# Eight instead of ten rows of w2 in every partition, and the other 352 rows as one load of 88 partitions

## The chip, the core and the metric

The kernel runs on one core of a Trainium2 chip. The metric is the device time of one execution in microseconds (us); the figure for the kernel before is the median of three timed runs, 344.06 us. A profile of one further execution gives a span (first to last instruction) and a trace with every instruction, every DMA packet and every increment of a DMA semaphore.

The engines are named as in the profile: PE multiplies matrices (PEld is its weight load), DVE, ACT and POOL are the vector, scalar and general engines, SP only issues DMAs here. "SPq" is the queue of DMAs that SP issues. A core has 16 DMA engines; one load is dealt out over several of them, each with its own share of the rows, and each of them reports to the load's semaphore when its share has landed.

## The reference

Two batch rows of one token pass through attention with a cache and through a small feed-forward block, and a gate mixes the two:

```python
q = (x @ wq)                       # [2, 4096] -> 32 heads of 128
scores = einsum(q, k_cache) * 128 ** -0.5        # k_cache [2, 32, 4096, 128]
o = einsum(softmax(scores), v_cache)             # v_cache [2, 32, 4096, 128]
a = o.reshape(2, 1, 4096) @ wo                   # wo [4096, 512]
h = maximum(B_x @ w1, 0)                         # w1 [512, 1376]
b = h @ w2                                       # w2 [1376, 512]
out = g * a + (1 - g) * b                        # g = sigmoid(sum(x * gate_w))
```

The weights and caches are bf16. Nearly all of the 145.43 MB that are read are the two caches (64 MB each, in MB of 2^20 bytes). In the kernel B_x is not read: the reference calls the feed-forward block with x too. The piece of work that matters here is `b = h @ w2`: its contraction runs over 1376 rows of w2, each of 512 bf16 numbers, that is 1 KB.

## The kernel before

**Loads.** SP issues all large loads in one order (lines 325 to 339): wq, w1, ten pieces of the key cache (L329), nine pieces of the value cache (L329, numbered v0 to v8, the last two of 4 MB), then the rows of w2 that are called `w2x` (L332, two loads), then wo in two parts (L334, L336), and last the shared part of w2 in three (L338: w2b, w2c, w2d). Each load waits for the region of SBUF that it overwrites; the w2 loads of L338 wait until the last piece but two of the value cache (v6) has been read by PE.

**w2 in two parts.** The contraction over 1376 rows is done 128 rows at a time. Rows 96 to 1375 are the shared part: 128 partitions by ten rows, loaded as seven, two and one row per partition (w2b, w2c, w2d). Rows 0 to 95 are `w2x`: 24 partitions by four rows, in two loads of 12 partitions each, at partitions 0 to 11 and 32 to 43. POOL has cleared the whole of `w2x` before (L710), so that the other partitions add nothing.

**The feed-forward rows.** `ffn_h` (L438) multiplies x with w1 in four column groups c and four depth steps t into one PSUM row block that DVE has cleared (L439): 16 matmuls of 320 columns for the shared rows, and 8 of 48 columns for the rows of `w2x` (groups 0 and 1 alone), the latter with the weights that PE already holds (`mm_held`, whose records stand under L477). `ffn_relu` (L457) transposes the result (L458, 448 columns) and writes `hT`, [128, 14, 2]: 14 columns of 128 contraction rows, ten for the shared part, four for `w2x`, for two batch rows.

**The end.** When the last value piece (v8) has been multiplied, `project(range(-4, 0))` (L663) adds the four `w2x` steps into PSUM, `o_gather`, `o_scale` and `o_turn` finish the heads, and `project(range(24))` multiplies with the first part of wo, 24 matmuls at L670 that wait for `wo0`. `pr_copy` (L675) copies this sum to SBUF. `last_rows` (L684) then adds, in groups of four matmuls (`fin_row`, L679): eight rows of the second part of wo (waiting for `wo1`), the copied sum, and the ten shared rows of w2, waiting for w2b before row 0, w2c before row 7 and w2d before row 9. Two DVE and two ACT copies (L698, L700) and one DMA store the result.

Of the kernel before, what the change touches and what calls it, by code (L numbers as in the profile page):

```python
# [3 lines left out]
dt = mybir.dt  # L4
# [6 lines left out]
DFF = 1376  # L11
# [5 lines left out]
REGION = {"A": 0, "Ah": HALF, "B": 2 * HALF, "Bh": 3 * HALF, "C": 4 * HALF}  # L17
# [104 lines left out]
def bass_gated_mix__gqa_block_cached__dense_activation_relu__decode_kernel(  # L122
# [18 lines left out]
    sb = nc.alloc_sbuf_tensor  # L141
# [11 lines left out]
    kv = sb("kv", [128, 5 * HALF], dt.bfloat16)  # L153
    xTw = sb("xTw", [128, 4, 32], dt.bfloat16)
    qrow = sb("qrow", [128, 2, 4, 128], dt.bfloat16)
    wreg = kv[:, REGION["C"]:REGION["C"] + HALF]
    w1 = kv[:, REGION["B"]:REGION["B"] + 4 * DFF]
    w2 = kv[:, REGION["Ah"]:REGION["Ah"] + 10 * 512].rearrange("p (r n) -> p r n", n=512)
    kt = sb("kt", [128, NKT, 2048], dt.float32)
    kt16 = kt[:, :, :].rearrange("p k n -> p (k n)").bitcast(dt.bfloat16).rearrange(  # L160
        "p (k g r par s two) -> p k g r par s two", k=NKT, g=2, par=2, s=16, two=2)
# [10 lines left out]
    w2x = kt_late[:, 13824:15872].rearrange("p (j n) -> p j n", n=512)  # L172
# [14 lines left out]
    s4 = sb("s4", [32, 4, 128], dt.bfloat16)  # L187
    O_sb = sb("O_sb", [32, 2, 128], dt.bfloat16)
    oW = sb("oW", [128, 32, 2], dt.bfloat16)
    hT = sb("hT", [128, 14, 2], dt.bfloat16)  # L190
    out_sb = sb("out_sb", [2, 512], dt.bfloat16)
    hrowT = kt[:, 2, 0:448]

    PSF = nc.alloc_psum_tensor("PS", [128, 4096], dt.float32)
    PSB = PSF[:, :].bitcast(dt.bfloat16)
# [3 lines left out]
    def psf(p0, p1, c0, n):  # L199
        return PSF[p0:p1, c0:c0 + n]  # L200

    BANK = 512
# [4 lines left out]
    QR_B = 2  # L207
    QT_B = 4
    G_C0 = MISC + 64
    HR_C0 = 6 * BANK - 320  # L210
    XT_B0 = 2 * (MISC + 400)
    L_C0 = MISC + 96
    O_C0 = MISC + 128
# [7 lines left out]
    sem = {n: nc.alloc_semaphore("sem_" + n) for n in names}  # L221
# [9 lines left out]
    def marker(name):  # L231
        m = mk.get(name)
        if m is None:
            m = _Marker()
            mk[name] = m
        return m
# [29 lines left out]
    def dve(fn, waits=(), signal=None, dwaits=()):  # L266
        P.add("dve", fn, waits=[marker(w) for w in waits], signal=marker(signal) if signal else None, dwaits=dwaits)
# [4 lines left out]
    def pe(fn, waits=(), signal=None, dwaits=()):  # L272
        P.add("pe", fn, waits=[marker(w) for w in waits], signal=marker(signal) if signal else None, dwaits=dwaits)
# [5 lines left out]
         waits=["c_i16z"], signal="c_i16")  # L279
# [8 lines left out]
         waits=["c_s1"], signal="c_s2")  # L288
    pool(lambda g: g.affine_select(out=sell_odd, in_=sell_odd, pattern=[[4, 8], [32, 4]],
                                   compare_op=ALU.is_ge, fill=0.0, base=3, channel_multiplier=-1),  # L290
         waits=["c_s2"], signal="c_sell")
# [3 lines left out]
         waits=["c_m1"], signal="c_m2")  # L295
    pool(lambda g: g.affine_select(out=mask8[:], in_=mask8[:], pattern=[[16, 8]],
                                   compare_op=ALU.is_ge, fill=0.0, base=15, channel_multiplier=-1),
         waits=["c_m2"], signal="c_mask8")
# [3 lines left out]
         waits=["c_s4z"], signal="c_s4")  # L302
# [2 lines left out]
    wq_in = A_wq.rearrange("(p t) n -> p (t n)", t=4)  # L305
    w1_in = B_w1.rearrange("(p t) f -> p (t f)", t=4)
    wo_in = A_wo.rearrange("(p r) n -> p (r n)", r=32)
    w2_in = B_w2[96:1376, :].rearrange("(p r) n -> p r n", r=10)
    w2x_in = B_w2[0:96, :].rearrange("(a i e j) n -> a e i (j n)", a=2, i=4, e=3)
    k_rows = A_k_cache.rearrange("b h s d -> (b h s) d")  # L310
    v_rows = A_v_cache.rearrange("b h s d -> (b h s) d")

# [7 lines left out]
    def sp(fn, waits=(), dwaits=()):  # L320
        P.add("sp", fn, waits=waits, dwaits=dwaits)
# [5 lines left out]
    for kind, n, u, halves, region in pieces:  # L327
        sp(lambda e, kind=kind, n=n, u=u, halves=halves, region=region:
           e.dma_start(piece_sb(halves, region), piece_in(kind, u, halves)).then_inc(landed[kind, n][0], 16),  # L329
           waits=[marker(m) for m in predecessor[kind, n]])  # L330
    for a in range(2):
        sp(lambda e, a=a: e.dma_start(w2x[32 * a:32 * a + 12, :, :].rearrange("p j n -> p (j n)"), w2x_in[a]).then_inc(sem["w2x"], 16),  # L332
           waits=[marker("c_w2x")])
    sp(lambda e: e.dma_start(wreg[:, 0:512 * WO_CUT], wo_in[:, 0:512 * WO_CUT]).then_inc(sem["wo0"], 16),  # L334
       waits=[marker(holder["C"][0])])
    sp(lambda e: e.dma_start(wreg[:, 512 * WO_CUT:HALF], wo_in[:, 512 * WO_CUT:HALF]).then_inc(sem["wo1"], 16))  # L336
    for name, r0, r1 in (("w2b", 0, 7), ("w2c", 7, 9), ("w2d", 9, 10)):
        sp(lambda e, name=name, r0=r0, r1=r1: e.dma_start(w2[:, r0:r1, :], w2_in[:, r0:r1, :]).then_inc(sem[name], 16),  # L338
           waits=[marker(holder["Ah"][0])])
    sp(lambda e: e.dma_start(out.rearrange("b s n -> (b s) n"), out_sb[:, :]).then_inc(sem["out"], 16),  # L340
# [56 lines left out]
    def x_rows(e, out, c, t, rhs, held):  # L397
        if held:
            return mm_held(e, out, xTw[:, t, :], rhs, t == 0, t == 3, (128, 32), (0, 32 * c))
        return e.matmul(out, lhsT=xTw[:, t, :], rhs=rhs, start=(t == 0), stop=(t == 3), tile_position=(0, 32 * c))  # L400
# [35 lines left out]
            q_place(k)  # L436

    def ffn_h():  # L438
        dve(lambda v: v.memset(psf(0, 128, HR_C0, 448), 0.0), signal="dve_h0")  # L439
        for t in range(4):  # L440
            for c in range(4):
                def fn(e, t=t, c=c):
                    rhs = w1[:, t * DFF + 96 + 320 * c:t * DFF + 416 + 320 * c].rearrange("p (i j) -> p j i", j=10)
                    out = psf(32 * c, 32 * c + 32, HR_C0, 320).rearrange("p (j i) -> p j i", j=10)
                    return x_rows(e, out, c, t, rhs, False)
                first = t == 0 and c == 0
                pe(fn, dwaits=([(sem["w1"], 16)] if first else []), waits=(["dve_h0"] if first else []))
                if c < 2:
                    def fnx(e, t=t, c=c):
                        rhs = w1[:, t * DFF + 48 * c:t * DFF + 48 * c + 48].rearrange("p (i e j) -> p j e i", i=4, e=3)  # L450
                        out = psf(32 * c, 32 * c + 32, HR_C0 + 320, 128).rearrange("p (j k) -> p j k", j=4)[:, :, 0:12].rearrange(
                            "p j (e i) -> p j e i", e=3)
                        return x_rows(e, out, c, t, rhs, True)
                    pe(fnx)
        P.ops["pe"][-1].marker = marker("pe_h")

    def ffn_relu():  # L457
        dve(lambda v: v.transpose(out=hrowT, in_=psf(0, 128, HR_C0, 448)), waits=["pe_h"], signal="dve_hrT")  # L458
        for b in range(2):
            dve(lambda v, b=b: v.tensor_scalar(out=hT[:, :, b], in0=hrowT[:, b:448:32], scalar1=0.0,  # L460
                                               scalar2=gm[:, b:b + 1], op0=ALU.max, op1=ALU.mult),
                waits=["dve_hrT", "dve_gm"], signal=f"dve_h{b + 1}")

# [200 lines left out]
    def project(rows):  # L664
        for r in rows:
            t = r % 4
            lhsT, rhs = (hT[:, 14 + r, :], w2x[:, t, :]) if r < 0 else (oW[:, r, :], wreg[:, r * 512:(r + 1) * 512])
            dw = {-4: [(sem["w2x"], 32)], 0: [(sem["wo0"], 16)]}.get(r, [])
            waits = {-4: ["dve_h2", "dve_pr0"], 0: ["dve_oW"]}.get(r, [])
            pe(lambda e, t=t, r=r, lhsT=lhsT, rhs=rhs: e.matmul(psf(32 * t, 32 * t + 2, PR_C0, 512), lhsT=lhsT, rhs=rhs,  # L670
                                                               start=(r < 0), stop=(r >= WO_CUT - 4), tile_position=(0, 32 * t)),
               dwaits=dw, waits=waits, signal=("pe_pr" if r == WO_CUT - 1 else None))
# [4 lines left out]
    def fin_row(first, last, lhsT, rhs, dw, waits, signal):  # L677
        for c in range(4):
            pe(lambda e, c=c: e.matmul(psf(32 * c, 32 * c + 2, FIN_C0, 128), lhsT=lhsT, rhs=rhs[:, c * 128:(c + 1) * 128],  # L679
                                       start=first, stop=last, tile_position=(0, 32 * c), skip_group_check=True),  # L680
               dwaits=(dw if c == 0 else []), waits=(waits if c == 0 else []), signal=(signal if c == 3 else None))

    def last_rows():
        for r in range(WO_CUT, 32):  # L684
            fin_row(r == WO_CUT, False, oW[:, r, :], wreg[:, r * 512:(r + 1) * 512], [(sem["wo1"], 16)] if r == WO_CUT else [], [], None)
        fin_row(False, False, sel2[:, :], pr_sb, [], ["dve_pr", "dve_sel2"], None)
        for r in range(10):
            dw = {0: [(sem["w2b"], 16)], 7: [(sem["w2c"], 16)], 9: [(sem["w2d"], 16)]}.get(r, [])
            fin_row(False, r == 9, hT[:, r, :], w2[:, r, :], dw, [], "pe_fin" if r == 9 else None)

    def store():
        def piece(c):
# [10 lines left out]
    gate()  # L703
    q_proj()
    ffn_h()
    ffn_relu()
    for i in range(64):
        k_turn(i)
# [22 lines left out]
    v_unit(last)  # L731
    v_extract(last)
    project(range(-4, 0))
    o_gather(1, (last,))
    o_scale(1)
    o_turn()
    project(range(WO_CUT))
    pr_copy()
    last_rows()
    store()  # L740

# [31 lines left out]
```

## Time and profile before

| What | us |
|---|---|
| median of three runs (343.96 to 344.13) | 344.06 |
| profiled execution, device time | 344.31 |
| its span, first to last instruction | 343.0 |
| span in which the three w2 loads of L338 are under way, from the last issue | 319.32 to 340.92 |
| last four matmuls, copies, store, after that | 340.96 to the end |

Busy times over the span: PE 220.4, DVE 197.2, PEld 52.7, POOL 13.9, ACT 10.2 us. The mean traffic is 424 GB/s. No engine that computes is busy for more than 64% of the span; the DMA engines' row in the page's 40 slices has no slice under eight tenths but the last.

Two kinds of record in the trace are used below beside the page. The packet records give start, duration, size and queue of every DMA packet, but not the engine. The semaphore records give the time of every increment; a load that is dealt out over k engines shows k increments at landing times. In this profile an increment comes some 0.4 us after the last packet of its engine.

### The profile page before, as it was taken

How to read it: one execution, taken by the hardware profiler on the slowest of the kernel's cores; microseconds unless marked ns; L12 is line 12 of the kernel's file. 1: busy time of each engine (PE TensorE's matmuls, PEld its weight loads, DVE VectorE, ACT ScalarE, POOL GpSimd, SP SyncE). 2: the span in 40 equal slices, each digit the busy share in tenths (PEclk: the TensorE clock that was granted, in tenths of full speed). 3: DMA queues.
4: the chain of work that ended last, by engine and by line, in shares of the span. 5: the costliest groups of instructions: out<-in, count | busy, mean ns of one | idle time of the engine just before them, and what ended most of it. 6: DMA issues, size and time to landing. Idle time of an engine off the chain costs nothing.

```text
span 343.0 us, 2384 instructions
## 1 busy us (share of the span) xinstructions
PE 220.4 (64%) x1236; PEld 52.7 (15%) x764; DVE 197.2 (57%) x140; ACT 10.2 (3%) x30; POOL 13.9 (4%) x38
## 2 busy tenths in 40 slices
PE   0454629889969799799799463709073542809655
PEld 0110101111111111111111121102020110202312
DVE  0247249899889899698999496230606041110621
ACT  1060000000000000000000120000000000000000
POOL 6000000000000000000000200000000000000000
PEclk9986958999989999989899966967858595876968
DMA  8998989899999999898999999898989999999995
GB/s 314 451 495 367 489 367 489 374 481 436 420 466 390 429 428 481 374 489 371 485 420 436 451 405 468 382 481 374 481 382 481 420 436 451 405 420 432 412 418 213
DMA packets 3789, 145.50 MB, mean 424 GB/s; under 512 B 427, under 2 KB 560, under 8 KB 840
## 3 DMA queue, kind: packets, MB, share of 16 engines
q1 hardware_dynamic: 3778, 145.43, 98.4%
q8 instruction: 4, 0.07, 0.1%
q14 instruction: 1, 0.01, 0.0%
q10 hardware_dynamic: 6, 0.00, 0.0%
HBM read 145.43 MB, written 0.00 MB: 424 GB/s over the span
## 4 chain that ended last, share of the span: by engine, by line
DMA 59%; DVE 19%; PE 17%; issue 4%; ACT 0%; SPq 0%; DVEq 0%
DMA kv<-in_A_v_cache_dram 25%; DMA kv<-in_A_k_cache_dram 24%; DVE kt L471 16%; PE PS L477 7%; DMA kv<-in_B_w_dram 6%; PE PS L603 4%; DMA kv<-in_A_wq_dram 4%; PE PS L498 2%; PE PS L582 2%; PE PS L400 1%; DVE qrow L424 1%; DVE mpad L514 1%; ACT kt L526 0%; PE PS L484 0%; DVE kt L530 0%
## 5 line engine op out<-in xcount | busy, mean ns | idle before, releaser
L471 DVE STREAM_TRANSPOSE kt<-kv 128x2048 f32<-128x2048 f32 x64 | 141.2, 2274 | 24.5 <-DMA kv<-in_A_k_cache_dram 24.5
L498 PE MATMUL PS<-kt,qbuf 128*128 128x512 bf16 x256 | 107.0, 418 | 32.0 <-issue 27.2
L477 PE MATMUL PS<-kt,qbuf 128*128 128x512 bf16 x256 | 106.9, 418 | 0.0
L603 PE MATMUL PS<-kv,kt 128*64 128x512 bf16 x192 | 46.5, 462 | 56.7 <-DMA kv<-in_A_v_cache_dram 56.7
L615 DVE TENSOR_TENSOR kt<-PS,maskc 32x512 f32<-32x512 f32 (+1 forms) x21 | 14.5, 689 | 89.8 <-PE PS L477 82.2
L498 PEld LDWEIGHTS PS<-kt,qbuf 128*128 128x128 bf16 x256 | 25.9, 101 | 141.5 <-issue 141.5
L477 PE MATMUL PS<-kv,kt 128*64 128x512 bf16 x192 | 45.9, 456 | 0.0
L603 PEld LDWEIGHTS PS<-kv,kt 128*64 128x64 bf16 x192 | 14.9, 132 | 96.4 <-issue 96.4
L582 PE MATMUL PS<-kv,kt 128*32 128x512 bf16 x128 | 11.5, 522 | 10.3 <-DVE kt L543 7.3
L555 DVE TENSOR_TENSOR kt<-kt,mask 128x2048 bf16<-128x2048 bf16 (+1 forms) x10 | 16.1, 1654 | 0.0
L395 POOL TENSOR_TENSOR qbuf<-qs,mask 128x64 bf16<-128x64 bf16 x16 | 6.5, 406 | 162.2 <-PE PS L477 145.6
L627 DVE TENSOR_REDUCE kt<-kt 128x128 f32<-128x512 f32 x9 | 9.2, 1019 | 0.3
L526 ACT ACTIVATE kt<-PS,negm 128x512 bf16<-128x512 f32 x4 | 2.7, 685 | 172.8 <-DVE negm L522 172.8
L400 PE MATMUL PS<-kv,xTw 128*32 128x512 bf16 (+1 forms) x32 | 5.3, 693 | 3.5 <-DMA kv<-in_A_wq_dram 3.5
L582 PEld LDWEIGHTS PS<-kv,kt 128*32 128x32 bf16 x128 | 4.7, 125 | 16.3 <-DVE kt L543 7.8
L424 DVE CAST qrow<-PS 128x256 bf16<-128x256 f32 x2 | 2.6, 1508 | 5.7 <-PE PS L477 5.7
L643 PE MATMUL PS<-kt,selx 128*32 128x128 f32 x18 | 2.9, 293 | 4.0 <-DVE kt L627 3.0
L347 PE MATMUL PS<-ident,x_sb 3*128 3x3 bf16 x4 | 0.3, 167 | 8.2 <-DMA x_sb<-in_gate_w_dram 8.2
L350 DVE COPY xT<-PS 128x12 bf16<-128x12 bf16 x1 | 0.2, 171 | 8.5 <-PE PS L347 8.5
L700 ACT ACTIVATE out_sb<-PS 2x128 bf16<-2x128 f32 x2 | 0.5, 270 | 142.3 <-PE PS L679 142.2
L514 DVE TENSOR_REDUCE mpad<-PS 128x2 f32<-128x2048 f32 x1 | 2.3, 2291 | 3.1 <-PE PS L510 3.1
L477 PE MATMUL PS<-kv,xTw 128*32 128x512 bf16 (+1 forms) x24 | 3.7, 512 | 0.0
(78 smaller groups left out, 45.2 us busy)
## 6 DMA issues: line engine op xcount, KB each, us to landing
kv<-in_A_k_cache_dram SPq DMA_DIRECT2D x4, 4096.0 KB, 29.4
kv<-in_A_v_cache_dram SPq DMA_DIRECT2D x2, 4096.0 KB, 24.4
kv<-in_A_wq_dram SPq DMA_DIRECT2D x1, 4096.0 KB, 12.5
kv<-in_A_wo_dram SPq DMA_DIRECT2D x1, 3072.0 KB, 34.2
kv<-in_B_w_dram SPq DMA_DIRECT2D x1, 1376.0 KB, 15.3
kv<-in_A_wo_dram SPq DMA_DIRECT2D x1, 1024.0 KB, 36.2
kv<-in_B_w_dram SPq DMA_DIRECT2D x1, 896.0 KB, 21.4
kv<-in_B_w_dram SPq DMA_DIRECT2D x1, 256.0 KB, 21.7
```

Of the source, the lines that this page charges most:

```text
L395: pool(lambda g: g.tensor_tensor(out=out, in0=src, in1=mask, op=ALU.mult).then_inc(sem_q[k % 2], 1), waits=waits)
L400: return e.matmul(out, lhsT=xTw[:, t, :], rhs=rhs, start=(t == 0), stop=(t == 3), tile_position=(0, 32 * c))
L424: dve(lambda v, dst=dst, src=src: v.tensor_copy(out=dst, in_=src), waits=[f"pe_qr{half}"], signal=f"qrow{half}{e2}")
L471: dve(lambda v: v.transpose(out=dst, in_=pairs[:, h, 64 * a:64 * a + 64, :]).then_inc(sem_kt[i % SPAN], 1), waits=([f"pe_sc_{i - NKT}"] if ...
L477: return e.add_instruction(mybir.InstMatmult(start_tensor_calc=start, stop_tensor_calc=stop, tile_size=size, tile_position=at, ldweights=F ...
L498: ins = e.matmul(out, lhsT=lhsT, rhs=rhs, start=False, stop=False)
L514: dve(lambda v: v.tensor_reduce(out=mpad[:, 0:2], in_=psf(0, 128, 0, 4 * BANK).rearrange("p (par n) -> p par n", par=2), axis=AX.X, op=ALU ...
L555: ins = v.tensor_tensor(out=out, in0=src.unsqueeze(2).to_broadcast(shape), in1=mask8[:].unsqueeze(1).unsqueeze(3).to_broadcast(shape), op= ...
L582: ins = e.matmul(psf(32 * t, 32 * t + 32, V_BS[n] * BANK, 512), lhsT=v_weights(n)[:, j], rhs=rows[:, :, j, :], start=(j < 4), stop=(j >= n ...
L603: ins = e.matmul(out, lhsT=lhsT, rhs=rows[:, :, k, :], start=start, stop=stop, tile_position=(0, 64 * t))
L615: dve(lambda e: e.tensor_tensor(out=parts[p0:p1], in0=psf(p0, p1, bank * BANK, 512).rearrange("p (c d) -> p c d", c=4), in1=maskc[p0:p1].u ...
L627: dve(lambda e: e.tensor_reduce(out=X2[:, b, k, :], in_=parts.rearrange("p c d -> p d c"), axis=AX.X, op=ALU.add), waits=[f"dve_m{n}"], si ...
```

## The change

The shared part gets eight rows per partition (rows 352 to 1375), loaded as five, two and one. The other 352 rows come as one load of 88 partitions by four rows, partitions 0 to 87. The feed-forward matmuls follow: 16 of 256 columns, and 12 (in groups 0, 1, 2) of 128, 128 and 96 columns; `hT` has 12 columns instead of 14, and the last stage adds eight rows of w2 instead of ten.

```diff
-    w2 = kv[:, REGION["Ah"]:REGION["Ah"] + 10 * 512].rearrange("p (r n) -> p r n", n=512)
+    w2 = kv[:, REGION["Ah"]:REGION["Ah"] + 8 * 512].rearrange("p (r n) -> p r n", n=512)
...
-    w2_in = B_w2[96:1376, :].rearrange("(p r) n -> p r n", r=10)
-    w2x_in = B_w2[0:96, :].rearrange("(a i e j) n -> a e i (j n)", a=2, i=4, e=3)
+    w2_in = B_w2[352:1376, :].rearrange("(p r) n -> p r n", r=8)
+    w2x_in = B_w2[0:352, :].rearrange("(p j) n -> p (j n)", j=4)
...
-    for a in range(2):
-        sp(lambda e, a=a: e.dma_start(w2x[32 * a:32 * a + 12, :, :].rearrange("p j n -> p (j n)"), w2x_in[a]).then_inc(sem["w2x"], 16),
-           waits=[marker("c_w2x")])
+    sp(lambda e: e.dma_start(w2x[0:88, :, :].rearrange("p j n -> p (j n)"), w2x_in).then_inc(sem["w2x"], 16), waits=[marker("c_w2x")])
...
-    for name, r0, r1 in (("w2b", 0, 7), ("w2c", 7, 9), ("w2d", 9, 10)):
+    for name, r0, r1 in (("w2b", 0, 5), ("w2c", 5, 7), ("w2d", 7, 8)):
...
-        dve(lambda v: v.memset(psf(0, 128, HR_C0, 448), 0.0), signal="dve_h0")
+        dve(lambda v: v.memset(psf(0, 128, HR_C0, 384), 0.0), signal="dve_h0")
...
-                    rhs = w1[:, t * DFF + 96 + 320 * c:t * DFF + 416 + 320 * c].rearrange("p (i j) -> p j i", j=10)
+                    rhs = w1[:, t * DFF + 352 + 256 * c:t * DFF + 608 + 256 * c].rearrange("p (i j) -> p j i", j=8)
...
-                if c < 2:
+                if c < 3:
                     def fnx(e, t=t, c=c):
-                        rhs = w1[:, t * DFF + 48 * c:t * DFF + 48 * c + 48].rearrange("p (i e j) -> p j e i", i=4, e=3)
+                        n = min(32, 88 - 32 * c)
+                        rhs = w1[:, t * DFF + 128 * c:t * DFF + 128 * c + 4 * n].rearrange("p (i j) -> p j i", j=4)
...
-        dve(lambda v: v.transpose(out=hrowT, in_=psf(0, 128, HR_C0, 448)), waits=["pe_h"], signal="dve_hrT")
+        dve(lambda v: v.transpose(out=hrowT, in_=psf(0, 128, HR_C0, 384)), waits=["pe_h"], signal="dve_hrT")
...
-            dw = {-4: [(sem["w2x"], 32)], 0: [(sem["wo0"], 16)]}.get(r, [])
+            dw = {-4: [(sem["w2x"], 16)], 0: [(sem["wo0"], 16)]}.get(r, [])
...
-        for r in range(10):
-            dw = {0: [(sem["w2b"], 16)], 7: [(sem["w2c"], 16)], 9: [(sem["w2d"], 16)]}.get(r, [])
-            fin_row(False, r == 9, hT[:, r, :], w2[:, r, :], dw, [], "pe_fin" if r == 9 else None)
+        for r in range(8):
+            dw = {0: [(sem["w2b"], 16)], 5: [(sem["w2c"], 16)], 7: [(sem["w2d"], 16)]}.get(r, [])
+            fin_row(False, r == 7, hT[:, r, :], w2[:, r, :], dw, [], "pe_fin" if r == 7 else None)
```

More of the change, by code (lines that the diff above doesn't have):

```diff
@@ L189, in bass_gated_mix__gqa_block_cached__dense_activation_relu__decode_kernel @@
     oW = sb("oW", [128, 32, 2], dt.bfloat16)
-    hT = sb("hT", [128, 14, 2], dt.bfloat16)
+    hT = sb("hT", [128, 12, 2], dt.bfloat16)
     out_sb = sb("out_sb", [2, 512], dt.bfloat16)
-    hrowT = kt[:, 2, 0:448]
+    hrowT = kt[:, 2, 0:384]
     PSF = nc.alloc_psum_tensor("PS", [128, 4096], dt.float32)
@@ L209, in bass_gated_mix__gqa_block_cached__dense_activation_relu__decode_kernel @@
     G_C0 = MISC + 64
-    HR_C0 = 6 * BANK - 320
+    HR_C0 = 6 * BANK - 256
     XT_B0 = 2 * (MISC + 400)
@@ L442, in fn @@
                 def fn(e, t=t, c=c):
-                    rhs = w1[:, t * DFF + 96 + 320 * c:t * DFF + 416 + 320 * c].rearrange("p (i j) -> p j i", j=10)
-                    out = psf(32 * c, 32 * c + 32, HR_C0, 320).rearrange("p (j i) -> p j i", j=10)
+                    rhs = w1[:, t * DFF + 352 + 256 * c:t * DFF + 608 + 256 * c].rearrange("p (i j) -> p j i", j=8)
+                    out = psf(32 * c, 32 * c + 32, HR_C0, 256).rearrange("p (j i) -> p j i", j=8)
                     return x_rows(e, out, c, t, rhs, False)
@@ L447, in ffn_h @@
                 pe(fn, dwaits=([(sem["w1"], 16)] if first else []), waits=(["dve_h0"] if first else []))
-                if c < 2:
+                if c < 3:
                     def fnx(e, t=t, c=c):
-                        rhs = w1[:, t * DFF + 48 * c:t * DFF + 48 * c + 48].rearrange("p (i e j) -> p j e i", i=4, e=3)
-                        out = psf(32 * c, 32 * c + 32, HR_C0 + 320, 128).rearrange("p (j k) -> p j k", j=4)[:, :, 0:12].rearrange(
-                            "p j (e i) -> p j e i", e=3)
+                        n = min(32, 88 - 32 * c)
+                        rhs = w1[:, t * DFF + 128 * c:t * DFF + 128 * c + 4 * n].rearrange("p (i j) -> p j i", j=4)
+                        out = psf(32 * c, 32 * c + 32, HR_C0 + 256, 128).rearrange("p (j i) -> p j i", j=4)[:, :, 0:n]
                         return x_rows(e, out, c, t, rhs, True)
@@ L457, in ffn_relu @@
     def ffn_relu():
-        dve(lambda v: v.transpose(out=hrowT, in_=psf(0, 128, HR_C0, 448)), waits=["pe_h"], signal="dve_hrT")
+        dve(lambda v: v.transpose(out=hrowT, in_=psf(0, 128, HR_C0, 384)), waits=["pe_h"], signal="dve_hrT")
         for b in range(2):
-            dve(lambda v, b=b: v.tensor_scalar(out=hT[:, :, b], in0=hrowT[:, b:448:32], scalar1=0.0,
+            dve(lambda v, b=b: v.tensor_scalar(out=hT[:, :, b], in0=hrowT[:, b:384:32], scalar1=0.0,
                                                scalar2=gm[:, b:b + 1], op0=ALU.max, op1=ALU.mult),
@@ L666, in project @@
             t = r % 4
-            lhsT, rhs = (hT[:, 14 + r, :], w2x[:, t, :]) if r < 0 else (oW[:, r, :], wreg[:, r * 512:(r + 1) * 512])
-            dw = {-4: [(sem["w2x"], 32)], 0: [(sem["wo0"], 16)]}.get(r, [])
+            lhsT, rhs = (hT[:, 12 + r, :], w2x[:, t, :]) if r < 0 else (oW[:, r, :], wreg[:, r * 512:(r + 1) * 512])
+            dw = {-4: [(sem["w2x"], 16)], 0: [(sem["wo0"], 16)]}.get(r, [])
             waits = {-4: ["dve_h2", "dve_pr0"], 0: ["dve_oW"]}.get(r, [])
```

## The prediction

> **What bounds the kernel now.** I read the page's slices and its chain of waits first, because they say which resource ends last.
>
> ```profile
> DMA  8998989899999999898999999898989999999995
> q1 hardware_dynamic: 3778, 145.43, 98.4%
> DMA 59%; DVE 19%; PE 17%; issue 4%; ACT 0%; SPq 0%; DVEq 0%
> ```
>
> The DMA engines are busy from the first slice to the last but one, and transfers fill the largest share of the chain. SP issues early enough that their queue never runs dry. So a load's size matters only through the moment at which the last of the 16 DMA engines finishes its last share. The end of the chain in order of time shows this:
>
> ```profile
> 319.32 21.59 DMA kv<-in_B_w_dram
> 340.96 0.26 PE PS L679 x4
> 341.21 0.02 issue
> 341.24 0.28 DVE out_sb L698
> ```
>
> The last load of L338 (w2d) lands at 340.92, and only four matmuls, the copies and the store come after it. Next I cut the end into short windows (columns: PE, PEld, DVE, ACT, POOL busy, granted clock, DMA share, GB/s):
>
> ```profile
> 337.00:338.00 1.00, 1.00 (x16) 0.30 (x12) 0.00 (x0) 0.00 (x0) 0.00 (x0) 0.51 0.97 386
> 338.00:339.00 1.00, 0.64 (x40) 0.46 (x36) 0.69 (x1) 0.00 (x0) 0.00 (x0) 1.00 0.63 243
> 339.00:340.00 1.00, 0.36 (x12) 0.07 (x16) 0.00 (x0) 0.00 (x0) 0.00 (x0) 1.00 0.39 129
> 340.00:341.00 1.00, 0.85 (x40) 0.48 (x40) 0.00 (x0) 0.00 (x0) 0.00 (x0) 1.00 0.05 18
> ```
>
> The DMA share falls from 0.97 to 0.05 over three microseconds: the engines do not finish together. The semaphore records say by how much. w2d's sixteen increments come at 338.74 to 339.05 (eight), then 339.24, 339.65, 339.81, 340.01, 340.26, 340.56, 340.76 and 340.92. The end waits for the last one.
>
> **Why they are apart.** w2x's semaphore has only six landing increments, 326.25 to 327.30, three for each load: its 24 packets of 4,096 B went to three engines, four and four each. Linking packets end to start, they stand 0.156 us apart, so each of the three lost 8 x 0.156 = 1.25 us; they are the ones at 339.81, 340.01 and 340.26 (their wo0 increments, 334.17, 334.35, 334.62, come 7.31 us after 326.86, 327.04, 327.30). The three that finish last, 340.56 to 340.92, carry no w2x. They were already late when v8 landed (327.61, 327.81, 327.96, while eleven engines landed between 325.63 and 326.09). Their lateness began at the 16 KB packets of queue 8 (instructions) at 24.67, 209.61 and 323.12: after the third, a 32,768 B packet starting at 324.127 took 1.764 us instead of 1.214. Each fetch fell on another engine and cost it about 1.5 us for good.
>
> **The change, part by part.**
>
> *Feed-forward rows.* The columns are the same in sum: 16 x 320 + 8 x 48 = 16 x 256 + 4 x 352 = 5,504. There are four matmuls more. By the held 48-column row (268 ns each) they cost at most 4 x 0.27 = 1.1 us, at least nothing. This line covers it:
>
> ```profile
> 24.47 5.78 issue
> ```
>
> PE idles for 5.78 us before the first scores, because the first key piece lands only at 27.81. The shorter memset and transpose (448 to 384 columns; the transpose takes 0.65 us, so some 0.09 less) lie in the same gap. The third key piece overwrites w1 and waits for these matmuls, but its load stands behind 12 MB that land until about 47 us, while the matmuls end near 23. I take 0.
>
> *Issues.* SP issues one load instead of two at L332 (0.73 and 0.87 us before). It then waits 16.5 us for v6's last matmul, so this is 0; without that cover the one issue saved would be worth at most 0.87 us.
>
> *Last matmuls.* Two rows of four fall away. The 32 matmuls of the second wo part run from 337.92 to 338.57, 0.02 us each, so 0.16 us is saved, inside waits for w2b, w2c and w2d:
>
> ```profile
> PEld PS L679 <- DMA kv<-in_B_w_dram: 1.4, 3, 0.9
> PE PS L670 <- DMA kv<-in_A_wo_dram: 0.9, 1, 0.9
> ```
>
> The second line matters too: the 24 matmuls of L670 already wait for wo0's last increment (335.27). If wo0 lands d later, PE's copied sum is d later; it ends near 339.4 while w2b lands at 339.92, so 0.5 us of cover. Eight rows of w2 take 0.64 us after it, so PE would be done at 340.05 + d, and by the transfers at 340.56 + d, as w2 comes behind wo0 on the same engines. The transfers stay the bound. w2x itself is needed at 331.28, four microseconds after its landing, so d may reach 3 us before these matmuls wait.
>
> *Shared part.* Every engine's w2b packets shrink from 7 to 5 KB. On the last engine wo1, w2b, w2c and w2d land at 337.75, 339.92, 340.59 and 340.92, so a 7 KB packet takes 0.271, a 2 KB packet 0.084 us, and 0.187 us go to the 5,120 B between them. A 5 KB packet then takes 0.196, and eight of them save 8 x 0.075 = 0.60 us on every engine.
>
> *The 352 rows.* In this trace every load puts equally many packets on each engine that it uses. 88 rows divide equally over 11 engines, 8, 4 or fewer, not over 12 to 16; I take 11, eight rows each. [...]
>
> An engine among the eleven gets 8 x 0.156 = 1.25 us of w2x and loses 0.60: +0.65 against before. The three that had w2x already only gain 0.60. The other five gain 0.60. So all hangs on where the late engines stand. They are not among the three old ones; of the other 13, eight get the load. For the very last engine alone that is 8 of 13, 62%. If it is spared and the next (340.76) is not, the end is 340.76 + 0.65 = +0.49; if only the third (340.56) is hit, +0.29. All three spared has 10 of 286 by chance, or 3 of 11 if the fetches walk through neighbouring engines. The trace has no engine numbers, so I give it 27%.
>
> *Whose partitions.* In the loads of 128 rows all engines run side by side at 1.214 us per 32 KB. The old w2x ran at full rate as well, with partitions 0 to 11 and 32 to 43. No row shows many engines writing rows that in the loads beside them belong to another. Bound: no cost (1.25 us), or every packet shares its way half and half (2.50 us), and the late engine's own stream is shared by early engines' rows as well (another 1.25): +0.65, +1.90 or +3.15. The nearest row is the one where two transfers shared an engine, 1.764 for 1.214, a factor 1.45: 1.25 x 1.45 = 1.81 us, less 0.60, is +1.21. I take it. [...]
>
> **The sum** on the profiled span: 343.0 + 1.2 = 344.2, with the 1.3 us outside it 345.5. That execution is 0.25 above the median of the runs, so against 344.06 it is 345.3.
>
> **The rivals.**
>
> *A: eleven engines, the late one among them, no sharing.* +0.65: 344.7. For it: the old w2x packets kept their rate beside others' traffic. Against it: they wrote few rows.
>
> *B: the late engines are spared, and nothing is shared: not slower.* The place is the last engine's w2b; the price is -0.60, 343.5. It decides if all three late engines stand among the five without w2x. Then the next are the other engines with w2x, at most 339.65 + 0.65 = 340.30, just below 340.32. For it: five engines lag behind the eleven at v8, as many as are spared. Against it: nothing ties the fetches to those five.
>
> [...]
>
> *D: the load is dealt over all 16 after all*, five or six rows each: 0.78 to 0.94 less 0.60, so about 344.3. Against it: 88 does not divide.
>
> **How the numbers follow.** Chances: forecast 0.45 (own range 344.9 to 347.2), A 0.22, B 0.12, C 0.15, D 0.06. The late engine is hit in 0.67 of this and spared in 0.27. The range 343.4 to 346.6 takes in A to D and leaves out the worst fifth of the forecast case, some 0.1. Faster or slower by 0.2% (0.69 us, about what a measurement of this kernel can tell from no change) means below 343.37 or above 344.75. Slower: nearly all of the forecast (0.44), a third of A (0.08), a quarter of C (0.04): 0.56. Faster: a third of B, 0.04, rounded up to 0.05. The rest, 0.39, is no change.
>
> **What would show it.** w2x's semaphore should have eleven landing increments (sixteen: D; eight: another deal). Its packets should take 0.156 us apart without sharing and more with it; 4,096 B records near 0.16 throughout kill the forecast and leave A. w2d's last increment should be near 342.1 (A 341.6, B 340.3). w2b should take 0.6 us less per engine. The wait of L670 for wo0 should grow by what the last engine lost; if it does not, the late engines were spared. I am wrong in kind if the last matmuls start on something other than w2d, or if the instruction fetches move: with four more instructions ahead of it the fourth, now at 339.94 when most engines are done, could come earlier and hold an engine that still has w2 to bring.

## The result, and the profile after

| | median us | runs | ratio to the kernel before, 95% interval |
|---|---|---|---|
| before | 344.01 | 343.93 to 344.13 | |
| changed | 346.81 | 346.06 to 347.01 | 1.0077 (1.006 to 1.0094) |

The change costs 2.80 us. That is the direction that was forecast, but more than twice the size (+1.2), and above the range's upper end of 346.6. The profiled execution took 346.64 us with a span of 345.3. That is 2.3 more than the profile before, so the traces show 2.3 of the 2.8 us: the profile before lies 0.3 above the median of its kernel, this one 0.2 below.

The slices, the queue and the chain of waits of the changed kernel:

```profile
DMA  8998999999898998989999998999999999999995
q1 hardware_dynamic: 3847, 145.43, 98.4%
DMA 63%; DVE 19%; PE 15%; issue 2%; SPq 0%; ACT 0%; DVEq 0%
```

Nothing has changed in kind. The same bytes pass, the DMA engines are busy throughout, and the end is again a load of w2, as the end of the chain of the changed kernel shows in order of time (start, us, what):

```profile
317.77 25.40 DMA kv<-in_B_w_dram
343.17 0.04 issue
343.21 0.26 PE PS L677 x4
343.47 0.02 issue
343.50 0.28 DVE out_sb L696
```

w2d lands at 343.17 instead of 340.92, and the last four matmuls follow at once. The lost time is in two stretches right after the w2x load. First the kernel before, then the changed one (columns: PE, PEld, DVE, ACT, POOL busy, granted clock, DMA share, GB/s):

```profile
324.00:328.00 4.00, 0.64 (x2) 0.18 (x2) 0.34 (x1) 0.00 (x0) 0.00 (x0) 0.54 0.97 412
328.00:332.00 4.00, 3.66 (x36) 1.22 (x36) 0.49 (x1) 0.00 (x0) 0.00 (x0) 0.61 1.06 455
```

```profile
324.00:328.00 4.00, 0.00 (x0) 0.00 (x0) 0.00 (x0) 0.00 (x0) 0.00 (x0) 0.63 1.06 318
328.00:332.00 4.00, 2.96 (x32) 1.20 (x36) 0.00 (x0) 0.00 (x0) 0.00 (x0) 0.52 0.97 339
332.00:335.00 3.00, 0.93 (x14) 0.15 (x6) 2.10 (x3) 0.00 (x0) 0.00 (x0) 1.00 0.97 418
...
341.00:342.00 1.00, 1.00 (x43) 0.68 (x32) 0.69 (x1) 0.00 (x0) 0.00 (x0) 0.50 0.24 90
342.00:343.00 1.00, 0.79 (x36) 0.36 (x28) 0.00 (x0) 0.00 (x0) 0.00 (x0) 0.96 0.12 33
```

The DMA engines count as fully busy in these eight microseconds (shares of 1.06 and 0.97), yet they move 318 and 339 GB/s instead of 412 and 455. (412 - 318) x 4 + (455 - 339) x 4 GB/s times us is 840 KB, 2.0 us at 424 GB/s. A busy share close to one with fewer bytes means packets that take longer. The packet records say which:

```
packets                          before                 changed
4,096 B (w2x)            24: 159 median, 165 most    88: 266 median, 446 most   (ns)
24,576 B (wo, first part) none over 1,000, 925 most   37 of 128 over 1,000, 1,809 most
```

At the other end of this the wait of PE for the first part of wo grew from 0.9 to 2.9 us:

```profile
PE PS L668 <- DMA kv<-in_A_wo_dram: 2.9, 1, 2.9
```

### The profile page after: what moved, and what is told of

It reads as the page before. It is cut to its first block, busy times and chain, and to the rows that moved or that the text cites. A ratio compares the mean times of both kernels' runs of the same rounds, so it can differ in the third digit from the quotient of the medians.

```text
span 345.3 us, 2371 instructions
## 1 busy us (share of the span) xinstructions
PE 220.2 (64%) x1232; PEld 52.5 (15%) x756; DVE 197.1 (57%) x140; ACT 10.2 (3%) x30; POOL 13.9 (4%) x38
## 4 chain that ended last, share of the span: by engine, by line
DMA 63%; DVE 19%; PE 15%; issue 2%; SPq 0%; ACT 0%; DVEq 0%
DMA kv<-in_A_k_cache_dram 32%; DMA kv<-in_A_v_cache_dram 24%; DVE kt L469 17%; DMA kv<-in_B_w_dram 7%; PE PS L475 6%; PE PS L601 4%; PE PS L496 2%; PE PS L580 2%; DVE mpad L512 1%; ACT kt L524 0%; DVE kt L528 0%; DVE kt L541 0%; PE PS L508 0%; SPq L336 0%; DVE out_sb L696 0%
## 5 line engine op out<-in xcount | busy, mean ns | idle before, releaser
L496 PE MATMUL PS<-kt,qbuf 128*128 128x512 bf16 x256 | 105.6, 412 | 32.2 <-issue 21.0
L475 PE MATMUL PS<-kt,qbuf 128*128 128x512 bf16 x256 | 105.6, 413 | 0.0
L398 PE MATMUL PS<-kv,xTw 128*32 128x512 bf16 (+1 forms) x32 | 4.9, 629 | 3.5 <-DMA kv<-in_A_wq_dram 3.5
L668 PE MATMUL PS<-kv,oW 128*2 128x512 bf16 x24 | 2.7, 623 | 2.9 <-DMA kv<-in_A_wo_dram 2.9
```

The lines of the kernel that those rows point to most:

```text
L475: return e.add_instruction(mybir.InstMatmult(start_tensor_calc=start, stop_tensor_calc=stop, tile_size=size, tile_position=at, ldweights=F ...
L496: ins = e.matmul(out, lhsT=lhsT, rhs=rhs, start=False, stop=False)
```

## The experiments

All times of kernels below are medians. The kernel before, run beside each group on the same chip, had 343.97 (other35, other1113, part96, own8), 344.02 (own256, row256, nine7) and 344.09 (half35, even256); ratios and differences are against these. In the kernel before the w2x loads have a pattern: by the source pattern (`i=4`, `e=3`) share k of a load (k from 0) is four neighbouring partitions, 4k to 4k + 3 in the first load and 32 + 4k to 32 + 4k + 3 in the second, each load has three landing increments, and the packets took 159 ns. Partitions in this pattern are called an engine's "own" below, packets outside it "straying". Whether the loads of 128 partitions fill the same partitions from the same engines is not shown: the traces have neither partitions nor engine numbers, and where an expectation gives engines a number or partitions of their own, it assumes so. What follows shows whether the place matters.

### The same packets of the kernel before in other partitions (other35, other1113)

```diff
-        sp(lambda e, a=a: e.dma_start(w2x[32 * a:32 * a + 12, :, :]...
+        sp(lambda e, a=a: e.dma_start(w2x[12 + 32 * a:12 + 32 * a + 12, :, :]...
...
-                        out = psf(...)...[:, :, 0:12].rearrange(
+                        out = psf(...)...[:, :, 12:24].rearrange(
```

other1113 does the same with partitions 76 to 87 and 108 to 119, and computes these rows in groups 2 and 3.

> The kernel before with its 96 rows of w2x moved from partitions 0 to 11 and 32 to 43 to partitions 12 to 23 and 44 to 55; the same three engines, the same bytes. Theory (packets that one engine writes into partitions which the loads beside it fill from another engine share a way into SBUF with them): the 24 packets of 4,096 B take about 0.31 us instead of 0.159, the three engines end some 1.25 us later than in the kernel before, w2d's last increment is 0.2 to 1.2 us later, 344.2 to 345.2. Rival (only the number of bytes on an engine counts): packets 0.159, time 344.0 as before.

> The kernel before with its 96 rows at partitions 76 to 87 and 108 to 119. [...] If late engines stand there, they lose up to 1.25 us and the time is up to 345.3; if not, 344.2 to 344.7. Rival (only bytes count): 344.0.

Measured: other35 345.22, ratio 1.0034 (1.0022 to 1.0046); other1113 345.34, 1.0039 (1.0025 to 1.0053). The rival falls. Three engines still carry the load (w2x's semaphore has six landing increments in each), and not a byte is added, but the time grows by 1.25 and 1.37 us. The median 4,096 B packet takes 312 and 318 ns instead of 159. The last increment of w2d comes at 341.69 and 341.80 instead of 340.92. Both times lie 0.02 and 0.04 us above the most that the theory gave. The range for other1113 turned on whether late engines fill its partitions in the large loads, which no trace shows. Its time cannot tell either: in other35 engines that carry none of the load are slowed as well (last section). In the window of other35:

```profile
324.00:328.00 4.00, 0.00 (x0) 0.00 (x0) 0.00 (x0) 0.00 (x0) 0.00 (x0) 0.70 1.04 313
```

That is 313 GB/s at a share of 1.04, where the kernel before moved 412, for 96 KB in other partitions.

### The dose (half35)

```diff
-        sp(lambda e, a=a: e.dma_start(w2x[32 * a:32 * a + 12, :, :]...
+        sp(lambda e, a=a: e.dma_start(w2x[44 * a:44 * a + 12, :, :]...
```

half35 is the kernel before with only the second of its two w2x loads moved, 12 of the 24 packets, from partitions 32 to 43 to 44 to 55.

> [...] Theory (the price follows the packets that go astray): half of what moving both loads cost, 344.6 (344.3 to 344.9), and the first 12 packets at 0.159 us. Rival (any straying packet triggers the whole loss): 345.2.

Measured: 344.67, ratio 1.0016 (1.0007 to 1.0025), +0.58 against 1.25 for both loads. The first packets of the load that stayed take 159 ns, the last ones of the load that moved up to 328. Here the price followed the packets.

### The shared part alone (part96)

```diff
-    w2x_in = B_w2[0:352, :].rearrange("(p j) n -> p (j n)", j=4)
+    w2x_in = B_w2[0:96, :].rearrange("(a i e j) n -> a e i (j n)", a=2, i=4, e=3)
...
+    for a in range(2):
+        sp(lambda e, a=a: e.dma_start(w2x[32 * a:32 * a + 12, :, :]...
```

> The changed kernel with w2x cut to rows 0 to 95, loaded and placed as in the kernel before; rows 96 to 351 are left out of the sum. It shows the shared part alone. Both theories: 4,096 B packets at 0.159 us, w2b 0.60 us shorter on every engine, w2d's last increment near 340.3, 343.4. If it is 344.0, the shrinking of w2b is not on the path.

Measured: 343.44, ratio 0.9982 (0.9973 to 0.9991), -0.53 us. The 5,120 B packets take 196 to 207 ns (196 was worked out), and the median 4,096 B packet 159. The chain of waits, drawn back from the end, now runs through PE and wo and no longer names w2:

```profile
300.28 34.58 DMA kv<-in_A_wo_dram
334.86 0.14 issue
334.99 2.73 PE PS L670 x18
337.72 2.51 PE PS L679 x62
340.23 0.02 issue
```

That does not mean that w2 is off the path. The view follows PE as long as a matmul counts as busy, and the ends of matmuls are modelled: the matmuls on w2 are given 263 to 314 ns each here, at a granted clock of 0.50, and some 218 ns in the kernel before, at 1.00. So they cover short waits. The weight loads in front of them show these waits:

```profile
338.93 0.43 PEld L679 LDWEIGHTS PS<-kv,hT 128*2 128x2 bf16 x20 [0.31 <-DMA kv<-in_B_w_dram]
339.61 0.10 PEld L679 LDWEIGHTS PS<-kv,hT 128*2 128x2 bf16 x8 [0.24 <-DMA kv<-in_B_w_dram]
339.93 0.09 PEld L679 LDWEIGHTS PS<-kv,hT 128*2 128x2 bf16 x4 [0.21 <-DMA kv<-in_B_w_dram]
```

w2b, w2c and w2d land at 338.89, 339.57 and 339.88, each 0.04 to 0.05 us before its rows start, and the copy of the result starts 0.37 us after w2d's last increment (0.32 in the kernel before). So w2d still ends last. On the last engine its increment comes 2.55 us after that of wo1 instead of 3.17: that is the 0.60 that was worked out. Against the profile before, w2d lands 1.04 us earlier; the other 0.42 is there at wo1 already, and the profile before lies 0.3 above the median of its kernel.

### The same bytes on eight engines, in own partitions or in a row (own256, row256)

```diff
-    w2x_in = B_w2[0:352, :].rearrange("(p j) n -> p (j n)", j=4)
+    w2x_in = B_w2[0:256, :].rearrange("(a i e j) n -> a e i (j n)", a=2, i=4, e=8)   # own256: two loads of 32 partitions
+    w2x_in = B_w2[0:256, :].rearrange("(i e j) n -> e i (j n)", i=8, e=8)            # row256: one load of 64 partitions
```

Both are the changed kernel with rows 0 to 255 alone in w2x, 32 KB on each of eight engines; rows 256 to 351 are left out of the sum.

> [...] Theory: 4,096 B packets stay at 0.159 us; one of the three engines that a fetch made late carries w2x (the third latest, as in the changed kernel) and ends at 340.56 - 0.60 + 1.25 = 341.2; 344.3. Rival (the count of bytes on a late engine explains all of the loss): as slow as the changed kernel, 346.8.

> The same rows, the same bytes on the same eight engines, but as one load of 64 consecutive partitions, eight neighbours to an engine (rows 256 to 351 left out again). Theory: packets of 4,096 B near 0.3 us, 24,576 B packets of the first part of wo up to 1.6 us, 346.0 to 347.0. Rival: the same time as own256.

Measured: own256 344.39, ratio 1.0009 (1.0 to 1.0018); row256 346.94, 1.0087 (1.0073 to 1.0101). This pair settles the size. Both put 32 KB on eight engines (eight landing increments for each load), and by their source patterns each eighth reads the same rows of w2 in both; what differs is the partitions that it fills, and one load instead of two. The times differ by 2.55 us. The windows of own256, then of row256:

```profile
324.00:328.00 4.00, 0.46 (x8) 0.20 (x12) 0.00 (x0) 0.00 (x0) 0.00 (x0) 0.61 1.01 429
328.00:332.00 4.00, 3.57 (x36) 1.06 (x28) 0.77 (x2) 0.00 (x0) 0.00 (x0) 0.53 1.02 437
```

```profile
324.00:328.00 4.00, 0.28 (x2) 0.00 (x0) 0.00 (x0) 0.00 (x0) 0.00 (x0) 0.50 1.04 328
328.00:332.00 4.00, 2.88 (x28) 1.09 (x32) 0.00 (x0) 0.00 (x0) 0.00 (x0) 0.50 0.97 358
```

In own256 every 4,096 B packet takes 159 to 171 ns and no packet of wo over 927; in row256 the median is 246 and the longest 540 for w2x, and 49 of 128 packets of wo take over 1,000 ns. In both, the chain of waits is again drawn through PE and wo (landing at 336.08 and 338.39), but as in part96 the last rows wait for w2d: it lands at 341.11 and 343.40, and the copy of the result starts 0.37 us later in each.

### An even deal over all sixteen (even256)

```diff
-    w2x_in = B_w2[0:352, :].rearrange("(p j) n -> p (j n)", j=4)
+    w2x_in = B_w2[0:256, :].rearrange("(p j) n -> p (j n)", j=4)
...
-    sp(lambda e: e.dma_start(w2x[0:88, :, :]...
+    sp(lambda e: e.dma_start(w2x[0:64, :, :]...
```

> The same 256 rows as in own256 and row256 (rows 256 to 351 left out), as 64 partitions by four rows in plain order, which deals them evenly: 16 KB on each of 16 engines, seventeen increments of w2x's semaphore or sixteen. [...] Theory: packets near 0.3 us, all first packets of wo stretched, 1.2 to 2.5 us above the even deal without straying: 345.2 to 346.5. Rival (only bytes per engine count): -0.60 + 0.62 = 0, 344.0, better than own256.

Measured: 345.97, ratio 1.0053 (1.0039 to 1.0067). Sixteen landing increments: all engines carry 16 KB. It is 1.58 us slower than own256 (1.51 when each is set against the kernel before beside it), which loads half of them with twice as much. The median w2x packet takes 272 ns. Here it mattered more where the packets went than how evenly they were dealt.

### Two ways to do the change in own partitions (own8, nine7)

```diff
+    w2y_in = B_w2[0:192, :].rearrange("(i e j) n -> e i (j n)", i=4, e=8)
+    w2x_in = [w2y_in[:, :, 0:2560], B_w2[192:352, :].rearrange("(i e j) n -> e i (j n)", i=4, e=8)]   # own8
+    w2e_in = w2y_in[:, :, 2560:3072]
...
+    w2_in = B_w2[224:1376, :].rearrange("(p r) n -> p r n", r=9)                                      # nine7
+    w2x_in = B_w2[0:224, :].rearrange("(a i e j) n -> a e i (j n)", a=2, i=4, e=7)
```

> Eight shared rows and the other 352 on engines 0 to 7 alone: 320 rows as two loads of 32 partitions by five rows (partitions 0 to 31 and 32 to 63), 32 as a load of 32 partitions by one row. By bytes it is worse than the changed kernel: 44 KB instead of 32 KB on the engines that carry it. Theory: each of these engines writes only partitions that are its own in the large loads, so packets keep their rate (5,120 B near 0.2 us), no other engine is slowed, and with the late engines spared the end is 0.6 us earlier, 343.4 (345.1 if one of the late engines is among the eight). Rival (only bytes count): the carrying engines end 0.45 us later than in the changed kernel, 346.8 or more.

> Nine shared rows and 224 rows on engines 0 to 6, 32 KB each, in two loads of 28 partitions at 0 and 32. Packets at 0.159 us by the theory. w2b loses one row, 0.30 us on every engine. If the third late engine is not among 0 to 6 the end is 0.30 us earlier, 343.7; if it is, 340.56 - 0.30 + 1.25 = 341.5, 344.6.

In own8 one of the five rows of w2x in each partition enters the sum twice in place of another; loads and matmuls are as many as for the full sum. Measured: own8 345.02, ratio 1.0029 (1.0019 to 1.0038); nine7 344.77, 1.002 (1.0011 to 1.0029). Both came out at the theory's second value (345.1 and 344.6), that of a late engine among the carrying ones. Both are faster than the changed kernel, although own8 puts 44 KB on each carrying engine instead of 32: its 5,120 B packets of w2x take 196 to 205 ns throughout. That speaks against the count of bytes as the cause once more. But neither is faster than the kernel before, and the records say why. own8's w2d comes between 340.07 and 340.39 on six of its eight carrying engines, and at 341.36 and 341.88 on two that were already late at v8. On two of nine7's seven it comes at 340.83 and 341.32; their v8 ended at 326.44 and 326.90, and w2x followed, while the two latest (326.97 and 327.03) went on with wo. So one of the three engines that a fetch made late is among the seven that nine7 uses. The kernel before puts its extra rows on three engines, none of them late.

## Why the prediction was off, by its own steps

**What bounds the kernel, right.** The last increment of w2d sets the end before and after (340.92 and 343.17; the copy of the result starts 0.32 us later in both), and the engines' spread is made of w2x and the fetches. The sign of being wrong by a moved fetch did not appear: the fourth came at 342.66 instead of 339.94, later and not earlier.

**Feed-forward rows, issues, last matmuls, at nothing: borne out by the trace.** In the changed kernel PE is done with the feed-forward rows before 22.83 us (22.97 before) and then still waits 5.2 us (5.8 before) until the first key piece is transposed. SP still waits 16.1 us (16.5 before) for v6's last matmul. The last rows still wait for w2c and w2d. None of the three was tried alone.

**Shared part, right.** 0.196 us for a 5 KB packet was estimated, and 196 to 207 ns were measured. -0.60 was forecast; part96 shows -0.62 between wo1 and w2d on the last engine, and -0.53 in the time.

**The deal, right.** w2x's semaphore has eleven landing increments in the changed kernel, from 327.75 to 331.06.

**Which engines, right in kind.** The late engines are hit in part. Among the five last at v8 in the changed kernel, the two latest (their last v8 packets end at 327.82 and 328.12) go on with a 24,576 B packet of wo, so they carry no w2x. The next (327.59) goes on with eight 4,096 B packets until 329.95. In the prediction's terms this is the case of the third engine, +0.29 alone, where the sum took +0.65. own256, whose w2x packets kept 159 to 171 ns, came to +0.37, close to that +0.29. So the sum was 0.36 too high here, and the miss in the next step is larger than the total shows. In the chances, 8 of 13 takes the three engines that had w2x before to be among the eleven, and 3 of 11 takes the eleven to be neighbours; no run shows either, and the changed kernel's trace shows two of the three latest spared.

**Whose partitions: the step that failed, by its size and by its reach.** The prediction took the factor 1.45 from the row in which two transfers shared an engine, 1.81 us for the late engine's eight packets, and so 0.56 us for sharing. Measured, the packets of the hit engine took 444, 355, 239, 246, 316, 301, 262 and 213 ns, 2.35 us from first to last, a factor 1.88: near the half-and-half bound, and 1.10 us of sharing instead of 0.56.

That was about half of it. The prediction charged sharing to the packets of w2x alone in its sum, and to the late engine's other packets only in its upper bound; v8 and wo had no term. The runs show that packets of v8 and wo in flight beside w2x pay too, and on all engines: even the earliest increment of wo's first part comes at 334.90 instead of 333.03. The hit engine, the third latest in both kernels, ended v8 at 327.59 instead of 327.11, and its eight packets of wo's first part took 7.69 us instead of 7.30. With 0.48 for v8, 2.35 for w2x, 0.39 for wo and 0.6 less for the shorter w2b its share of w2d comes 2.61 us later, at 343.17 instead of 340.56, and ends the kernel alone. Sharing is 1.97 us of that.

C, with the late engines spared but held up by others' packets, had a chance of 0.15; no run shows whose partitions these packets entered, nor how many of them. What the runs showed in its place: the two latest engines carry nothing, yet their last packets of wo's first part end at 336.07 and 336.25, where the latest two before had 1.4 us less (334.7 and 334.8, eight packets of 0.914 us after 327.36 and 327.52): 0.5 to 0.6 us of that is in v8, the rest in their first two packets of wo, 1.548 and 1.233, 1.556 and 1.115 us. In row256 only eight of the engines carry the load, and still the six fastest engines' first part of wo lands at 334.60 to 334.83 instead of 333.13 to 333.56 in own256. The pair of kernels prices the whole at 2.55 us.

**The sum, term by term**, from differences of medians: shared part -0.53 (part96; predicted -0.60), 32 KB on eight engines +0.95 (own256 less part96; predicted +1.25), the straying +2.55 (row256 less own256; predicted +0.56), the remaining 96 rows and eleven engines instead of eight -0.13 (changed less row256; no term). Each kernel is compared with the one before it in this row, so that the terms must add up to the change (+2.84 against 2.80); what they show is the size of each.

**The bound of the sharing.** The upper end, +3.15, held the result; the chances cut the range at 346.6 below it. The half-and-half bound, +1.90, gives 346.0. The packets agree with its doubling (159 to 312 ns in other35); it has no term for engines elsewhere, which are held up as well (the first nine packets of wo in other35, 1.33 to 1.66 us instead of 0.91).

**PE behind wo, right.** The prediction gave PE 0.5 us of cover behind wo's landing and kept the transfers as the bound. In the changed kernel the cover was nearly gone: the copied sum was added from 341.81 on, and w2b landed at 342.18 (338.93 and 339.92 before). Still the last rows waited for w2d, there and in every experiment: the copy of the result starts 0.32 to 0.43 us after w2d's last increment.

## What to carry to other kernels

When the DMA engines bound a kernel, price an odd-shaped load by the partitions that it fills, not by its bytes alone: here 96 KB in 24 packets cost 1.25 us more in partitions 12 to 23 and 44 to 55 than in 0 to 11 and 32 to 43 (other35), and 256 KB in consecutive partitions, eight to an engine, cost 2.55 us more than in the pattern of the kernel before (row256 less own256), because packets in flight beside them slowed down too (in row256 49 of 128 packets of wo took over 1,000 ns, in own256 none over 927). That pattern kept its packets at 159 to 171 ns with eight engines as well (own256); other patterns at this rate were not shown. Where the trace shows a pattern at full rate, keep such a load in it, even if the order of the rows and the code around it become awkward. And look at the spread of a semaphore's increments before dealing out extra work: which engines are late decides what an uneven load costs.

## What the runs showed of the hardware that was not expected

In other35 a few straying packets slowed engines that have no part in them. Three engines write 96 KB into partitions 12 to 23 and 44 to 55, but all of the first nine packets of wo, which start between 325.27 and 325.61, take 1.33 to 1.66 us instead of 0.91. By 328.2 the rate is back. Summed over the packets of v7 and v8, of wo's first part and of w2x, the excess over the kernel before is 4.3, 12.8 and 2.6 us, 19.7 in all, or 1.2 us for each of 16 engines, close to the 1.25 us that the kernel lost. What the engines share on the way was not shown.

In both profiles an instruction fetch of 16 KB cost the DMA engine on which it fell about 1.5 us for good: in the kernel before, 1.016 us for the fetch at 323.12 and 0.55 for the packet behind it. Each of the first three fell on another engine: three engines end v8 late, at 327.11, 327.36 and 327.52 before, at 327.59, 327.82 and 328.12 in the changed kernel. In the changed kernel the third fetch came at 321.61, and the packet behind it took 1.762 us. The engine on which it fell is the one that then carried w2x and ended last: a fetch 24 us before the end of a kernel of 345 us decided, together with w2x, which engine the end waited for.
